# An mLSTM cell followed by a GELU MLP: weights converted by three VectorE operations from 16-bit fields, the first down projection as seven block products, and a new order for the first stage

## The chip, the cores and the metric

The kernel runs on one core of one Trainium2 chip. The metric is the time of one execution on the device in microseconds (us), the median of several runs. The engines named below are TensorE (PE; its weight loads are PEld), VectorE (DVE), ScalarE (ACT), GpSimd (POOL) and SyncE (SP), whose queue issues all the transfers (DMAs).

## The reference, cut to what matters

The gated recurrence is computed for 4 batches, 8 heads, 768 positions and 40 channels. Its output, turned to 3072 tokens of 320 channels, goes through two matrices with an exact GELU between them. The two weight matrices arrive as 64-bit floats; everything else is 32-bit.

```
for t in range(S):                                  # S = 768
    m_new = max(f_gate[t] + m, i_gate[t])
    C = exp(f_gate[t] + m - m_new) * C + exp(i_gate[t] - m_new) * outer(v[t], k[t])
    n = exp(f_gate[t] + m - m_new) * n + exp(i_gate[t] - m_new) * k[t]
    y[t] = sigmoid(o_gate[t]) * (C @ q[t]) / max(|n . q[t]|, 1)
x   = y as (3072, 320)
out = gelu(x @ w_in) @ w_out                        # w_in 320 x 2048, w_out 2048 x 320, float64
```

## The kernel before, in words

The 768 positions are cut into NCH = 6 chunks of 128. A chunk of all 4 batches makes 512 tokens, and these pass through three steps: the cell (class `Cell`, once for each chunk and batch), the up projection with GELU into the hidden tile `g` (2048 x 512), and the down projection (`po`) to the output. Nothing is scheduled automatically: every engine works through its own queue in the order in which the program issues. That order is written out by hand as strings of step names, `FRONT` for the first stage and `DOWN` for each later one, and `play` (L946) runs the steps of a string one by one.

FRONT covers everything up to the end of the first down projection: the gates, the cells of chunks 0 and 1, the conversion of all weights, and the up and down projections of chunk 0. Its names stand for these steps; small letters are for chunk 0 and capitals for chunk 1, with the batch as the number:

- E and N compute the gates of chunk 1 and of chunks 2 to 5 (`gates_of`, L249: scans and differences on VectorE) and turn them with TensorE (`gates_turned`, `decays_of`).
- P fetches a weight piece (`fetch`, L337), L loads q and k, O loads v and the output gate, and B loads the running maxima of a batch (`load_M`).
- w (exponentials on ScalarE, L433), t (transposes of k and q, L482), s (scores, L508, multiplied on VectorE, L511), c (carry, L546), v (values, L622), g (sigmoid of the output gate, L439), y (finish, L635 to L640) and x (transposes of the result, L657, copied to `first_x`, L662) are the parts of a cell. `twice` (L646) copies the last 64 channels into a tile that all batches share.
- A and U are the up projection of the first and the second 256 tokens, in blocks of two hidden tiles (`up_step`, L753, its matmuls L762 and L768, its GELU L772). F is the first down projection: 16 steps, one for each 128 rows of w_out, each with 4 matmuls of 128x320 (L869).
- k (`warm`, L213) and I (`keep_clock`, L381) issue matmuls whose results nobody reads (L216, L387).

The weights are cut into 26 pieces, 10 of w_in (512 values in each partition) and 16 of w_out (320). They pass through NB = 4 shared buffers `bits`. Step K (`conv_one`, L349) splits a piece on VectorE into exponent (L358), upper significand (L363) and whole significand (L365), while two ScalarE operations make the power of two (L360, L361). Step J (`conv_two`, L367) puts in the sign (L372), multiplies (L375), and fetches the piece that is four further on.

Later stages compute the up projection in a split form (L817, L828) and the down projection as seven block products (`down_steps`, L879, matmuls L892): each of the two 256-token halves of `g`, times halves of w_out, with sums of weight blocks (`weight_sum`, L723, 32 operations L731 in all) and sums of hidden blocks (`hidden_sums`, L744) in place of the eighth product. Before, the weight sums were made in the second stage, because the first one didn't need them.

Buffers `sums` for the hidden sums share their tag with `bits`. The queue of SP issues in program order too, so a transfer whose buffer isn't free holds up all that are behind it.

Of the kernel before, what the change touches and what calls it, by code (L numbers as in the profile page):

```python
# [12 lines left out]
U32 = mybir.dt.uint32  # L13
AF = mybir.ActivationFunctionType
OP = mybir.AluOpType

P = 128

I23 = 2.0 ** 23
# [9 lines left out]
    I2 O0 g0 L0 P0 L1 E k1 t0 P1 P2 k7 w0 N k2 w1 O1 K L2 Q s0 O3 w2 q D k2 d P3 t1 w3 c0 L3 J v0 t2 K K y0 s1 I7 v1  # L29
    I8 O2 J g1 L4 I5 c1 K I1 I2 y1 s2 x0 t3 B4 O4 B5 g2 J x1 s3 v2 c2 L5 y2 H T0 x2 G0 v3 g3 c3 K y3 M1 J L6 J A x3  # L30
    M0 K W0 O7 K A O6 O5 J M2 W1 S0 C0 K J J T1 U U K L7 V0 K T2 r J J A G2 K G1 Y0 W2 S1 K M3 C1 A J S2 J K W3 K V1 C2
    Y1 T3 J J U U S3 V2 K K J G3 J Y2 C3 X0 K V3 J K F J F K K B8 F J K F F J K F F F R0 X1 J J K F J F K X2 F J K F
    J Y3 K F R1 J F Z B9 B10 F X3 R2 Z R3 F p"""
# [6 lines left out]
def kernel(  # L40
# [179 lines left out]
    nc.vector.memset(e_hi, 1151.0 * I23)  # L220
    nc.vector.memset(e_lo, 255.0 * I23)

# [74 lines left out]
    def second_gates():  # L297
        gates_of(1, 2)
        nc.sync.dma_start(out=M_d[0], in_=M[:, 1])
        gates_turned((a[:, 1:2], aT[:, 1:2]))  # L300
        decays_of(0, 2, 0, 1)

    def later_gates():
        gates_of(2, NCH)
        nc.sync.dma_start(out=M_d[1:].rearrange("c p l -> p c l"), in_=M[:, 2:])
        gates_turned((a[:, 2:], aT[:, 2:]))
        decays_of(2, NCH - 1, 1, NCH - 1)
# [3 lines left out]
    for name, w in (("in", moe_w_in), ("out", moe_w_out)):  # L311
        rows, cols = w.shape
        w_src[name] = bass.AP(tensor=dataclasses.replace(w.tensor, shape=[rows, 2 * cols], dtype=U32), offset=0,
                              ap=[[2 * cols, rows], [1, 2 * cols]])
# [3 lines left out]
    w_cols = lambda e, f, n: slice(DFF * e + 2 * f, DFF * e + 2 * (f + n))  # L318
# [18 lines left out]
    def fetch(i):  # L337
        if i >= len(pieces):
            return
        src, dst = pieces[i]  # L340
        n = sum(x.shape[0] * x.shape[1] for x in src) // (2 * P)
        bits[i] = raw.tile([P, WP, 2], U32, name="bits", tag="bits", bufs=NB)[:, 0:n, :]
        to = bits[i].rearrange("p n two -> p (n two)")
        row = col = 0
        for x in src:
            nc.sync.dma_start(out=to[row:row + x.shape[0], col:col + x.shape[1]], in_=x)
            row, col = (row + x.shape[0]) % P, col + (x.shape[1] if x.shape[0] == P else 0)

    def conv_one(i):  # L349

        if i < len(pieces):
            n = bits[i].shape[1]
            lo, hi = bits[i][:, :, 0], bits[i][:, :, 1]
            s = sig[i] = raw.tile([P, WP], F32, name="sig", tag="sig")[:, 0:n]
            p = pow2[i] = raw.tile([P, WP], F32, name="pow", tag="pow")[:, 0:n]
            su, pu = s.bitcast(U32), p.bitcast(U32)

            nc.vector.tensor_scalar(out=pu, in0=hi, scalar1=20, scalar2=0x7FF,  # L358
                                    op0=OP.logical_shift_right, op1=OP.bitwise_and)
            nc.scalar.activation(out=p, in_=pu, func=AF.Relu, scale=-I23, bias=e_hi)  # L360
            nc.scalar.activation(out=pu, in_=p, func=AF.Relu, scale=-1.0, bias=e_lo)  # L361

            nc.vector.tensor_scalar(out=su, in0=hi, scalar1=0xFFFFF, scalar2=0x100000,  # L363
                                    op0=OP.bitwise_and, op1=OP.bitwise_or)
            nc.vector.scalar_tensor_tensor(out=s, in0=lo, scalar=2.0 ** -32, in1=su, op0=OP.mult, op1=OP.add)  # L365

    def conv_two(i):  # L367

        if i < len(pieces):
            hi, p = bits.pop(i)[:, :, 1], pow2.pop(i)  # L370
            pu = p.bitcast(U32)
            nc.vector.scalar_tensor_tensor(out=pu, in0=hi, scalar=0x80000000, in1=pu,  # L372
                                           op0=OP.bitwise_and, op1=OP.bitwise_or)
            dst, s = pieces[i][1], sig.pop(i)
            nc.vector.scalar_tensor_tensor(out=dst, in0=s, scalar=2.0 ** -20, in1=p, op0=OP.mult, op1=OP.mult)  # L375
            fetch(i + NB)
# [16 lines left out]
    class Cell:  # L393
# [138 lines left out]
        def carry(self, b):  # L532

            c, n = self.c, self.c * B + b
            qT = self.qT.pop(b)
# [96 lines left out]
        def finish(self, b):  # L632
# [9 lines left out]
            if len(self.finished) == len(self.turned) + 1:  # L642
                self.twice(b)
# [4 lines left out]
        def turn_y(self, b):  # L648
# [10 lines left out]
            if len(self.finished) > len(self.turned):  # L659
                self.twice(b + 1)  # L660
# [74 lines left out]
    class Hidden:  # L735


        def __init__(self, summed):
            self.t = gp.tile([P, NF, TG], F32, name="g", tag="g")
            if summed:  # L740
                self.s1, self.s2 = [[raw.tile([P, HF // 2, HT], F32, name="sums", tag="bits", bufs=NB)
                                     for _ in range(2)] for _ in range(2)]
# [10 lines left out]
    def up_step(g, sets):  # L753

        banks = []
        for k, (i0, i1, t0, t1) in sets:
            banks.append([ps_mm.tile([P, i1 - i0, t1 - t0], F32, name="pu", tag="ab"[k % 2]) for e in range(2)])
# [16 lines left out]
    ups, tags_next = [], []  # L774

    def first_up_steps(h):

        def step(k):
            ups.append((len(ups) + len(tags_next) % 2, (2 * k, 2 * k + 2, HT * h, HT * h + HT)))
            if len(ups) == 2:  # L780
                first_up()

        return [lambda k=k: step(k) for k in range(HF // 2)]

    def first_up():
        if len(ups) == 1:
            tags_next.append(1)
        if ups:
            up_step(first_g, ups)
        ups.clear()  # L790

# [66 lines left out]
    def first_down_steps(g):  # L861
        po = []

        def row(f):

            if f == 0:
                po.extend(ps_mm.tile([P, DM], F32, name="po", tag="ab"[b // 2]) for b in range(B))
            for b in range(B):
                nc.tensor.matmul(po[b], g.t[:, f, b * L:(b + 1) * L], w_out[:, f, :], start=(f == 0),  # L869
                                 stop=(f == NF - 1))  # L870
                if f == NF - 1:
                    if b % 2 == 0:
                        o_sb = outp.tile([P, 2, DM], F32, name="o_sb", tag="o_sb")
                    nc.scalar.copy(out=o_sb[:, b % 2, :], in_=po[b])
                    send(0, b, o_sb[:, b % 2, :])

        return [lambda f=f: row(f) for f in range(NF)]

    def down_steps(c, g):  # L879
        A = lambda e, h: lambda j, t: g.t[:, HF * e + j, HT * h + t * L:HT * h + (t + 1) * L]  # L880
        Sm = lambda s: lambda j, t: s[j // (HF // 2)][:, j % (HF // 2), t * L:(t + 1) * L]
# [53 lines left out]
        def p4(pb, tiles=slice(0, 2)):  # L935
            add(block(1, 0)[:, tiles], pb, block(1, 0)[:, tiles])
            for t in range(2)[tiles]:
                send(c, 2 + t, o_sb[1][:, t, :])

        todo = ((A(0, 0), Bm[0][0], 0, True, p1), (Sm(g.s2), T[2], 1, True, p6),  # L940
                (A(1, 0), Bm[1][0], 0, False, p2), (Sm(g.s1), T[1], 2, True, p5),
                (A(0, 1), T[3], 3, True, p7), (A(1, 0), Bm[1][1], 2, False, p3),
                (A(1, 1), T[4], 3, False, p4))
        return [lambda x=x, t=t: product(*x[0:4], t, x[4]) for x in todo for t in range(2)], sum_late

    def play(order, steps):  # L946

        for word in order.split():
            if word[0] not in "AU":
# [65 lines left out]
```

## Time and profile before

| what | value |
|---|---|
| runs of the kernel before | 479.59, 479.76 and 481.75 us, median 479.76 |
| span of the profiled execution | 479.6 us (it isn't timed apart from that; the span lies 0.2 us below the median of the runs) |
| instructions | 13238 |
| engines busy | PE 469.0, PEld 405.3, DVE 349.1, ACT 222.1, POOL 74.7 us |
| mean granted TensorE clock | 0.999 |
| data moved | 44.57 MB in 170428 packets |

The span runs from the first to the last instruction. An engine's busy time is the time in which it had an instruction under way; matmuls overlap, so a busy PE need not be one at its peak. The chain of waits follows the work that ended last back from the end of the program, and what lies on it sets the time.

### The profile page before, as it was taken

To read this page: it belongs to the slowest core of one execution; us is meant where nothing else is said; L and a number is where in the kernel's file an instruction comes from. 1 tells how busy PE (TensorE), PEld (TensorE's weight loads), DVE (VectorE), ACT (ScalarE), POOL (GpSimd) and SP (SyncE) were. 2 spreads that over 40 slices of the span, in tenths; PEclk is the share of its full clock that TensorE was granted. 3 is DMA by queue.
4 is the path that set the end of the run, shared out by engine and by line. 5 is a ranking of instruction groups with operands and counts; after the bars stand their busy time and mean duration, and the time that the engine had idled before them with its cause. 6 is when DMAs were issued, how large, how long until landed. Compare 5 with 4: busy or idle time off the path is not lost.

```text
span 479.6 us, 13238 instructions
## 1 busy us (share of the span) xinstructions
PE 469.0 (98%) x5380; PEld 405.3 (85%) x5380; DVE 349.1 (73%) x762; ACT 222.1 (46%) x477; POOL 74.7 (16%) x104
## 2 busy tenths in 40 slices
PE   7899999999999999999999999999999999999997
PEld 7787888777777998977999977998977899977997
DVE  7899789797879989956598846597765589724321
ACT  6987999844532942113952113952104862112300
POOL 3002200000020215300224300315300114000000
PEclk9999999999999999999999999999999999999999
DMA  9997966279420348551357551358551350100001
GB/s 176 201 225 172 200 164 149 77 197 194 133 30 4 40 84 189 77 113 12 42 104 178 72 108 15 37 88 178 73 122 15 38 88 8 55 1 0 1 1 55
DMA packets 170428, 44.57 MB, mean 93 GB/s; under 512 B 156448, under 2 KB 163904, under 8 KB 170368
## 3 DMA queue, kind: packets, MB, share of 16 engines
q1 hardware_dynamic: 170368, 43.73, 46.0%
q8 instruction: 42, 0.69, 0.6%
q14 instruction: 18, 0.15, 0.1%
HBM read 39.58 MB, written 4.13 MB: 91 GB/s over the span
## 4 chain that ended last, share of the span: by engine, by line
PE 93%; DVE 3%; SPq 1%; DMA 1%; issue 1%; ACT 0%; DVEq 0%
PE po L892 33%; PE pu L817 24%; PE po L869 7%; PE pu L828 6%; PE pu L762 6%; PE ph L622 4%; PE ps L524 2%; PE px L657 2%; PE pu L768 2%; PE pf L579 2%; PE pf L590 1%; PE ps L508 1%; SPq L148 1%; PE pf L546 1%; PE pt L482 1%
## 5 line engine op out<-in xcount | busy, mean ns | idle before, releaser
L892 PE MATMUL po<-w_out,g 128*128 128x160 f32 x640 | 92.1, 301 | 0.0
L892 PEld LDWEIGHTS po<-w_out,g 128*128 128x128 f32 x640 | 87.6, 190 | 2.3 <-ACT g L832 1.8
L832 ACT ACTIVATE g<-pu 128x512 f32<-128x512 f32 x80 | 40.8, 614 | 52.9 <-PE pu L828 52.8
L892 PE MATMUL po<-w_sums,sums 128*128 128x160 f32 x320 | 47.7, 303 | 0.0
L892 PEld LDWEIGHTS po<-w_sums,sums 128*128 128x128 f32 x320 | 44.1, 190 | 0.7
L817 PE MATMUL pu<-x_hi,w_in_hi 128*128 128x512 f32 x160 | 41.7, 403 | 0.0
L817 PE MATMUL pu<-x_lo,w_in_lo 128*128 128x512 f32 x160 | 40.6, 395 | 0.0
L433 ACT ACTIVATE W<-W,aT 128x128 f32<-128x128 f32 x128 | 39.2, 389 | 0.1
L667 ACT ACTIVATE x_hi<-px 128x384 fp32r<-128x384 f32 x20 | 9.8, 489 | 63.1 <-PE px L657 63.1
L817 PEld LDWEIGHTS pu<-x_hi,w_in_hi 128*128 128x128 f32 x160 | 28.5, 188 | 9.4 <-ACT g L832 4.1
L749 DVE TENSOR_TENSOR sums<-g 128x512 f32<-128x512 f32 x20 | 13.8, 688 | 30.8 <-ACT g L832 30.8
L817 PEld LDWEIGHTS pu<-x_lo,w_in_lo 128*128 128x128 f32 x160 | 30.1, 188 | 7.2
L869 PE MATMUL po<-w_out,g 128*128 128x320 f32 x128 | 35.2, 433 | 0.0
L869 PEld LDWEIGHTS po<-w_out,g 128*128 128x128 f32 x128 | 24.0, 190 | 9.6
L832 ACT ACT_TABLE_LOAD x5 | 6.4, 1283 | 55.1 <-DMA blocks<-in_k_dram 27.6
L817 PE MATMUL pu<-x_all,w_mid 128*128 128x512 f32 x80 | 31.6, 395 | 0.0
L817 PE MATMUL pu<-x_all,w_in_mid 128*128 128x512 f32 x80 | 31.6, 395 | 0.0
L721 DVE TENSOR_TENSOR w_in_mid<-w_in_hi,w_in_lo 128x512 fp32r<-128x512 f32 x20 | 13.8, 688 | 24.5 <-PE pu L817 24.5
L445 POOL MEMSET g<- 32x1024 f32 x8 | 7.6, 945 | 148.1 <-ACT W L433 122.5
L407 POOL TENSOR_SCALAR_AFFINE_SELECT W<-W 128x1024 f32<-128x1024 f32 (+2 forms) x20 | 21.1, 1068 | 53.7 <-DMA W<-M_d 40.9
L762 PE MATMUL pu<-first_x,w_in 128*128 128x256 f32 x128 | 28.9, 381 | 0.0
L905 DVE TENSOR_TENSOR o_sb<-po,o_sb 128x320 f32<-128x320 f32 (+1 forms) x27 | 12.5, 463 | 20.8 <-PE po L892 16.7
(183 smaller groups left out, 908.0 us busy)
## 6 DMA issues: line engine op xcount, KB each, us to landing
W<-M_d SPq DMA_DIRECT2D x16, 512.0 KB, 5.4
bits<-in_moe_w_in_dram SPq DMA_DIRECT2D x20, 256.0 KB, 4.3
bits<-in_moe_w_out_dram SPq DMA_DIRECT2D x16, 320.0 KB, 3.3
ob<-in_o_gate_dram SPq DMA_DIRECT2D x24, 160.0 KB, 3.6
out_dram<-o_sb SPq DMA_DIRECT2D x24, 160.0 KB, 2.1
vb<-in_v_dram SPq DMA_DIRECT2D x14, 160.0 KB, 4.9
kb<-in_k_dram SPq DMA_DIRECT2D x14, 160.0 KB, 5.1
g<-M_d SPq DMA_DIRECT2D x4, 512.0 KB, 4.4
```

What stands on the lines that cost most here:

```text
L407: nc.gpsimd.affine_select(out=x, in_=x, compare_op=OP.is_ge, fill=1.0e30, base=base, pattern=[[0, H], [1, x.shape[2]]], channel_multiplier=-1)
L433: nc.scalar.activation(out=W[n][:, h, :], in_=src, func=AF.Exp, scale=-1.0, bias=aT[:, self.c, r:r + 1])
L622: nc.tensor.matmul(ph[r, h, :], Pm[:, h, r], vb[turn_of(n)][:, h, :], start=True, stop=True)
L721: nc.vector.tensor_tensor(out=w_mid[i], in0=w_hi[i], in1=w_lo[i], op=OP.add)
L749: nc.vector.tensor_tensor(out=s1, in0=a21, in1=a22, op=OP.add)
L762: nc.tensor.matmul(banks[-1][e][:, i - i0, :], in_tile(i, x)[:, e, i % 2 * P:(i % 2 + 1) * P], first_x[:, x, t0:t1], start=(x == 0 and i = ...
L817: nc.tensor.matmul(pus[i][e], w[k][:, e, i * P:(i + 1) * P], x[:, k, :], start=(n == 0 and k == 0), stop=False, skip_group_check=True)
L828: nc.tensor.matmul(pu[e], w[r, i // 2, i % 2 * P:(i % 2 + 1) * P], x[r, NX, :], start=False, stop=(n == 2), skip_group_check=True)
L832: nc.scalar.activation(out=g.t[:, HF * e + i, :], in_=pu[e], func=AF.Gelu, scale=4097.0)
L869: nc.tensor.matmul(po[b], g.t[:, f, b * L:(b + 1) * L], w_out[:, f, :], start=(f == 0), stop=(f == NF - 1))
L892: nc.tensor.matmul(bank[at][:, i, :], lhs(j, t), rhs(j), start=(first and i == 0 and j == 0), stop=(i == n - 1 and j == HF - 1), skip_grou ...
L905: nc.vector.tensor_tensor(out=to, in0=pb, in1=x, op=OP.add)
```

## The change

All three parts lie in the first stage, and what they need of the second is taken out there.

The conversion. A piece is now fetched as 16-bit fields, two bytes past the start of its buffer. In this way the top field (sign, exponent and 4 bits) can be read as one signed 16-bit number, and the next 32 bits as one 32-bit word. Four steps do a piece: a (`conv_zero`: one ScalarE operation), b (`conv_low`: one VectorE operation with one source, written straight into the destination), K (`conv_one`: a VectorE operation with two sources, then one on ScalarE) and J (`conv_two`: one VectorE operation that joins the two parts). VectorE has three operations for each piece instead of five, and ScalarE two, as before. `fetch` is no longer part of J: P appears in FRONT for each piece.

The first down projection. It uses `down_steps` as all later stages do: 14 steps F with 8 matmuls of 128x160 each, instead of 16 with 4 of 128x320. The weight sums (l) and the hidden sums (e, n) of the first stage are now made in FRONT.

The order. Gates are computed chunk by chunk (Ga, Na2 to Na5), loads are split (Lk, Lq, Lv, Lo), `twice` is a step of its own (z, zz), the batches of chunk 0 run in the order 0, 1, 3, 2, the first up blocks run as A, A, U, U, A, and k and I are gone from FRONT; the 12 matmuls of `warm` ahead of FRONT stay. (A 32-bit matmul leaves two records in the trace.)

The core of the diff:

```diff
-    I2 O0 g0 L0 P0 L1 E k1 t0 P1 P2 k7 w0 N k2 w1 O1 K L2 Q s0 O3 w2 q D k2 d P3 t1 w3 c0 L3 J v0 t2 K K y0 s1 I7 v1
-    I8 O2 J g1 L4 I5 c1 K I1 I2 y1 s2 x0 t3 B4 O4 B5 g2 J x1 s3 v2 c2 L5 y2 H T0 x2 G0 v3 g3 c3 K y3 M1 J L6 J A x3
...
+    Ga Na2 P0 Lk0 Lq0 Lv0 Na3 Lk1 a w1 Na4 t0 Lq1 Lv1 Lo3 Lk3 w0 Lo0 Gc Gd s0 t1 b Lq3 w3 Gb D c0 c1 Lo2 Lo1 Lv2 g0
+    Na5 Lk2 s1 Lv3 g2 K Nc v0 g1 v1 t3 y0 g3 Lq2 P1 z0 w2 s3 P2 t2 P3 B4 y1 a v3 c2 Nd b P4 J K x0 d z1 s2 x1 Q a a v2
+    Lk4 M0 b J K K Lv4 Lq4 P5 P6 W0 a y2 J q A z2 y3 T0 K b x2 c3 b z3 x3 J J S0 a K a P7 b J a b K K A P8 a P9 a b M2
+    Nb H P10 J J b b P11 K a K J b a P12 K a J J b K K b C0 V0 J P13 a P14 P15 U K J P16 b b b b a J Lq5 K Lk6 P17 P18
+    J a a Lq6 K K J a K b J a J K U P19 l a b P20 Lk5 l l l J K a P21 a b J K b b K Lv6 P22 P23 P24 P25 Lv5 B5 T2 J J
+    P26 l Lq7 l b a a K b Lo4 M1 K e A P27 Lo5 b b e Lo7 Lv7 Lk7 T1 J a a W1 J K K G3 e G0 F S1 l F e J J l l Y0 M3 C1
+    V1 r l G1 W2 S2 F T3 W3 Y1 F Lo6 C2 G2 V2 P28 S3 l l zz0 F Y2 C3 V3 Y3 P29 F X0 Z Z l F n zz1 l l l F R0 X1 zz2 F
+    B9 R1 X2 B10 zz3 F F F X3 R3 B8 R2 F F p"""
...
-        bits[i] = raw.tile([P, WP, 2], U32, name="bits", tag="bits", bufs=NB)[:, 0:n, :]
-        to = bits[i].rearrange("p n two -> p (n two)")
+        words = raw.tile([P, 2 * WP + 2], U32, name="bits", tag="bits", bufs=NB)
+        to = words.bitcast(U16)[:, 1:1 + 4 * n]
+        bits[i] = words[:, 1:1 + 2 * n].rearrange("p (n two) -> p n two", two=2)[:, :, 0], \
+            words.bitcast(I16)[:, 4:4 + 4 * n].rearrange("p (n four) -> p n four", four=4)[:, :, 0]
...
+    def conv_zero(i):
...
+            nc.scalar.activation(out=s, in_=top, func=AF.Relu, scale=-1.0, bias=e_lo)
...
+    def conv_low(i):
...
+            nc.vector.tensor_scalar(out=pieces[i][1].bitcast(U32), in0=bits[i][0], scalar1=2.0 ** -13, scalar2=2.0 ** 19 - 1.0,
+                                    op0=OP.mult, op1=OP.min)
...
     def conv_one(i):
...
-            nc.vector.tensor_scalar(out=pu, in0=hi, scalar1=20, scalar2=0x7FF,
-                                    op0=OP.logical_shift_right, op1=OP.bitwise_and)
-            nc.scalar.activation(out=p, in_=pu, func=AF.Relu, scale=-I23, bias=e_hi)
-            nc.scalar.activation(out=pu, in_=p, func=AF.Relu, scale=-1.0, bias=e_lo)
-            nc.vector.tensor_scalar(out=su, in0=hi, scalar1=0xFFFFF, scalar2=0x100000,
-                                    op0=OP.bitwise_and, op1=OP.bitwise_or)
-            nc.vector.scalar_tensor_tensor(out=s, in0=lo, scalar=2.0 ** -32, in1=su, op0=OP.mult, op1=OP.add)
+            nc.vector.scalar_tensor_tensor(out=s, in0=top, scalar=LOW, in1=s, op0=OP.max, op1=OP.subtract)
+            nc.scalar.activation(out=p.bitcast(I32), in_=s, func=AF.Identity, scale=2.0 ** 19, bias=e_hi)
...
     def conv_two(i):
...
-            nc.vector.scalar_tensor_tensor(out=pu, in0=hi, scalar=0x80000000, in1=pu,
-                                           op0=OP.bitwise_and, op1=OP.bitwise_or)
-            nc.vector.scalar_tensor_tensor(out=dst, in0=s, scalar=2.0 ** -20, in1=p, op0=OP.mult, op1=OP.mult)
-            fetch(i + NB)
+            nc.vector.tensor_tensor(out=dst, in0=pow2.pop(i).bitcast(U32), in1=dst, op=OP.bitwise_or)
...
-                nc.tensor.matmul(po[b], g.t[:, f, b * L:(b + 1) * L], w_out[:, f, :], start=(f == 0),
-                                 stop=(f == NF - 1))
...
+    def first_sums(f):
+        if f == 0:
+            first_g.sums()
+        hidden_sums(first_g, f, f + 2)
+    def weight_sums():
+        for n in range(1, 5):
+            yield from weight_sum(n)
+    def first_down():
+        yield from down_steps(0, first_g)[0]
+    def late_first():
+        for i in range(2):
+            a12 = first_g.t[:, HF + HF // 2 * i:HF + HF // 2 * (i + 1), 0:HT]
+            nc.vector.tensor_tensor(out=a12, in0=a12, in1=first_g.s2[i], op=OP.subtract)
...
-        up(g, weight_sum(1) + weight_sum(2) + weight_sum(3) if c == 1 else [], [lambda b=b: (steps["K"](b), steps["Q"](b)) for b in range(2)] if steps else [])
-        if c == 1:
-            later = weight_sum(4)
+        up(g, [], [lambda b=b: (steps["K"](b), steps["Q"](b)) for b in range(2)] if steps else [])
```

## The prediction

> **What bounds the kernel now.** I read the page first, for the engines' shares:
>
> ```profile
> PE 469.0 (98%) x5380; PEld 405.3 (85%) x5380; DVE 349.1 (73%) x762; ACT 222.1 (46%) x477; POOL 74.7 (16%) x104
> PE 93%; DVE 3%; SPq 1%; DMA 1%; issue 1%; ACT 0%; DVEq 0%
> ```
>
> The second line is the chain that ended last: 93% of the span is TensorE work, so the question is where TensorE is not yet on it, and what its part there consists of. The chain in order of time tells both:
>
> ```profile
> 26.37 1.21 DVE W L511 x2
> 27.62 1.02 PE ph L622 x28
> ...
> 40.87 3.65 PE pu L762 x16
> ...
> 92.89 0.63 issue
> 93.80 17.42 PE po L869 x64
> ...
> 111.56 4.31 PE po L869 x16
> 116.19 10.77 PE po L869 x40
> ...
> 127.29 2.16 PE po L869 x8
> 129.44 11.16 PE pu L817 x48
> ...
> 445.80 30.64 PE po L892 x224
> ```
>
> Up to 27.6 us the chain runs through gates, a transfer and VectorE. Then TensorE takes over; the first up block starts at 40.87, and the first stage ends at 129.44. In the 88.6 us between these two TensorE waits for almost nothing. The first down projection takes 17.42 + 4.31 + 10.77 + 2.16 = 34.7 us there, and the last line is the same product done as seven block products: 30.6 us.
>
> Then I read the engines by stretches of 10 us (length, then busy us of PE, PEld, DVE, ACT and POOL, the granted clock, the DMA share and GB/s):
>
> ```profile
> 10.00:20.00 10.00, 8.77 (x85) 6.72 (x84) 8.32 (x25) 8.35 (x28) 0.00 (x0) 1.00 1.04 191
> 20.00:30.00 10.00, 9.62 (x146) 8.42 (x148) 9.68 (x22) 9.37 (x22) 0.00 (x0) 1.00 1.01 216
> 30.00:40.00 10.00, 9.04 (x151) 7.90 (x151) 9.06 (x23) 6.19 (x14) 0.00 (x0) 1.00 1.06 257
> ```
>
> VectorE is the busy one here (it idles 2.9 of these 30 us), and part of TensorE's busy time is the unread matmuls. So ahead of the first up block VectorE's queue sets the time, and behind it TensorE does. VectorE's share is mostly conversion:
>
> ```profile
> L365 DVE SCALAR_TENSOR_TENSOR sig<-bits,sig 128x320 f32<-128x320 uint32 x16 | 7.9, 493 | 0.5
> L358 DVE TENSOR_SCALAR pow<-bits 128x320 uint32<-128x320 uint32 x16 | 5.1, 320 | 0.1
> ```
>
> In the timeline an instruction starts before its predecessor's recorded end, so I count from start to start: 0.24 us for an operation with one source on 320 values (0.33 on 512), 0.41 and 0.61 with two sources.
>
> **The first part, up to the first up block.** It now stands on TensorE behind cell 0's four scores and values (L511, L622), but ahead of carry 3 and transposes x2 and x3; its first half needs the second converted piece. What VectorE has queued up to that: it is at 6.6 us when the first chunk's gates are split, as before. Then five chunks of gates one by one, 6.6 us (the lone chunk took 6.62 to 7.96; the last lacks one operation; before, four were done together, and the five took 6.0); turned copies and decays 3.0; four scores of 1.20 = 4.8; two finishes of 1.56 with the shared copy = 3.4; three weighted values of 0.41 = 1.2; and of the conversion three b, two K and two J, 3 x 0.33 + 4 x 0.61 = 3.4. That is 22.4 us. For waits I add 3.0, the idle time of the stretches above, since the same ScalarE exponentials and sigmoids stand in between. So the first up block starts at 6.6 + 22.4 + 3.0 = 32.0 us instead of 40.9. Its second half needs the third piece: two K, one finish and one J more, 3.4 us, so 35.4; the first half takes 3.5, and nothing is lost. Without waits it would start at 29.0.
>
> The order of loads has fetch 0 ahead of k and q of batch 0; these 0.5 MB delay them by some 2 us at the 191 GB/s above. Scores 0 run at 16.7 us today and are due at about 12.5, behind exponentials that need the gates, so this hides; if it doesn't, it costs at most the 2 us.
>
> **The second part, from there to the stage's end.** TensorE had 88.6 us. The seven products take 30.6 instead of 34.7: -4.0. Transposes of chunk 1's batch 0 (1.02), x2 (0.36) and carry 3 (0.47), which stood ahead, now stand behind: +1.9. So 86.5 us, if VectorE follows. Two places where it doesn't:
>
> Carry 3 waits for the weighted values of batch 3, which VectorE reaches behind finish 3, a K, a b and small copies: 35.4 + 3.9 = 39.3; TensorE is there at 37.9. Cost 1.4 us; all of chunk 1 is queued behind it.
>
> The third block product needs sums over all of w_out and all hidden sums, so all 26 pieces must be through by then. From 35.4 on VectorE has 23 b (7 x 0.33 + 16 x 0.24), 22 K (6 x 0.61 + 16 x 0.41) and 23 J (7 x 0.61 + 16 x 0.41) = 27.2 us; twelve hidden sums of 0.61 = 7.3; sixteen weight sums, which took 0.245 each at L731, = 3.9; and cell work (finish 3, four weighted values, two scores, one carry and values, copies) = 8.6. That makes 47.0. From 40 to 130 us VectorE idled 13.6 of 90 us, but often with nothing urgent; I take 10% for its waits on ScalarE and TensorE, 4.7: 87.1 us. TensorE has 50.9 us of work between the two places, so it is there at 32.0 + 1.4 + 50.9 = 84.3 and waits 2.8. Behind that, 33 us of TensorE face 29 of VectorE (remaining sums, adds, cells, splits), so TensorE leads again.
>
> End of the stage: 32.0 + 86.5 + 1.4 + 2.8 = 122.7 instead of 129.4, a gain of 6.7 us.
>
> **The rest.** ScalarE keeps two operations a piece and loses table loads, because the GELUs stand together: 15 loads of 1.28 us in the first stage become 8. It isn't on the path, so I count nothing; it is cover for the steps a. The second stage loses its 32 weight sums from VectorE. It takes 72.8 us today, the third one 71.8 without them: a gain of 0 to 1.0, and I take 0.5. Later stages are unchanged.
>
> Sum: 479.6 - 6.7 - 0.5 = 472.4 us of span; the runs' median lies 0.2 above the span, so 472.6 us.
>
> **What the trace doesn't show.** Step b is arithmetic on every second 32-bit word. L358, of one source too and with the same stride, runs at 0.24 and 0.33; the upper bound is the two-source rows, 0.41 and 0.61. I take L358. Step K reads 16-bit numbers eight bytes apart; the nearest row is L365 (two sources, one strided), which I take for both ends.
>
> **Rivals.** *VectorE binds* (chance 0.18): b goes at the two-source pace. Then 3 x 0.28 ahead of the first block and 7 x 0.28 + 16 x 0.17 = 4.7 us behind it are added where VectorE is already last: 478.1 us. For it: VectorE's margin is gone. Against it: L358's row.
>
> *VectorE keeps up everywhere* (0.20): the two stalls of 1.4 and 2.8 us vanish, 468.4 us; without the start's waits too, 465.4. For it: TensorE lost almost nothing after 40.9 before, with 52 us of conversion on VectorE from start to start (10 x 2.5 + 16 x 1.7); now it is 33 (10 x 1.55 + 16 x 1.06).
>
> *The clock falls* (0.08), the case that ends slower. Steps k and I are gone, 28 unread matmuls (56 records) between 7.5 and 31 us. The granted clock is 1.00 in every stretch, but with them in place. The work of cell 0 on TensorE between 7.4 and 32 us comes to about 21 us at full clock; at half of it 21 us are added, of which the 4 us of gaps hide some, so up to 17. With half of the stretch at half clock the first up block moves by 8.5 us, to 40.5, and the time is 481.1. It decides from a shift of 7.2 us on. The Trainium skill, "TensorE: Matmul & The Clock Gate", Part 1, says that after an idle window of about 3.4 us the array runs at half its clock until such a window was busy; by that rule the case needs a gap of that length. Against it: by my sum 21 of 25 us are work, and the 12 of `warm` at the start remain.
>
> *The transfers slow down* (0.04): rows now land two bytes off a word. Rows of vb land four bytes off kb's alignment at 4.9 against 5.1 us, so no cost shows, but two bytes aren't shown. DMA is busy 100.8 of the first 130 us. The pieces are 10.5 MB, at 3.4 us a MB (the stretch from 100 to 110 us, mostly pieces: 1.89 MB in 6.4 us of busy time) 36 us. At twice that the stage can't end before 137 us: 487. It decides from a factor of 1.8.
>
> That the change doesn't do what it says I leave at no chance: the order of the instructions shows it.
>
> **How the numbers follow.** The forecast itself has 0.47 and spans 469.5 to 475.5. A remaining 0.03 is for waits in the new order that I overlooked, which make it slower. The measurement can tell some 0.5%, 2.4 us, from no change. Faster than 477.4: 0.47 + 0.20 + half of the first rival = 0.76. Same: the other half, 0.09. Slower: 0.08 + 0.04 + 0.03 = 0.15. The range reaches from 465.4 to past the first rival, 479.0.
>
> **What would show it.** In the new profile: first up block (L763) near 32 us, the third block product near 87, the second stage's first matmul near 123; the first down product's matmuls adding up to 30.6; b at 0.33 and 0.24 from start to start; clock 1.00 throughout. Wrong would be: a clock below 1 in the first 40 us, VectorE or a weight transfer as releaser for more than some 8 us of TensorE's waits behind the first up block, or a gap ahead of it past 36 us.

## The result, and the profile after

| what | before | forecast | after |
|---|---|---|---|
| median of the runs, us | 481.31 (20 runs, 479.52 to 482.83) | 472.6 | 479.39 (20 runs, 477.63 to 482.17) |
| span of the profiled execution | 479.6 | 472.4 | 478.2 (its own time: 480.07) |
| first up block starts | 40.87 | 32.0 | 31.15 |
| third block product starts | none | 87.1 | 87.97 |
| second stage starts | 129.44 | 122.7 | 126.44 |
| from there to the last stage's first matmul | 287.8 | 287.3 | 289.5 |

A block product is here one of the 14 steps F, two to each of the seven products; the third is the first one that needs sums. The starts of the stages and the 40.87 are read from the chain, the 31.15 and 87.97 from the timeline, which starts a group 0.1 to 0.4 us earlier (40.80, 129.04 and 126.17 us for the other three).

The ratio of the times is 0.9963 with a 95% interval of 0.9948 to 0.9979: about 0.4% faster, where 1.5% was forecast. The interval only just excludes no change, and of the forecast fall of 7.2 us (479.76 to 472.6) 1.9 came. The time lies 0.4 us above the top of the range.

The page of the changed kernel, first the engines, then the chain that ended last:

```profile
PE 460.5 (96%) x5420; PEld 405.4 (85%) x5420; DVE 338.2 (71%) x735; ACT 211.3 (44%) x468; POOL 75.7 (16%) x104
PE 62%; issue 17%; DVE 8%; ACT 7%; DMA 2%; POOL 2%; SPq 1%; POOLq 0%; DVEq 0%; ACTq 0%
```

TensorE's share of the chain falls from 93% to 62%. Not all of that is waiting: in the fifth stage the chain leaves TensorE at a single wait of 1.4 us, at 399 us, and runs for 63 us (from 336.8) through transfers, GpSimd and ScalarE, while TensorE was busy without a break up to that wait (61.0 us from 337 to 398). The plainer sign is that TensorE has 8.5 us less to do, but the span is only 1.4 us shorter: waits have taken the place of work. The waits of TensorE from 30 us up to the second stage say for whom (engine and line, the releaser, us in total, times, longest; one of the four for W, 0.2 us, lies just ahead of the first up block):

```profile
PE px L655 <- DVE y_rest L644: 3.0, 2, 2.7
PE ph L620 <- DVE W L509: 1.5, 4, 0.6
PE pf L544 <- DVE vw L493: 1.2, 1, 1.2
PE pu L763 <- ACT g L773: 0.7, 1, 0.7
```

In the kernel before this list had a single entry, of 0.6 us. The table by stretches of 10 us (busy us of PE, PEld, DVE, ACT and POOL, granted clock, DMA share, GB/s) puts the largest wait behind 110 us:

```profile
90.00:100.00 10.00, 9.44 (x168) 8.66 (x167) 9.70 (x29) 5.42 (x17) 1.11 (x1) 1.00 0.63 123
100.00:110.00 10.00, 9.15 (x145) 8.64 (x141) 9.02 (x27) 3.13 (x6) 0.74 (x1) 1.00 0.32 52
110.00:120.00 10.00, 7.78 (x57) 7.57 (x58) 6.27 (x17) 0.98 (x2) 0.00 (x0) 1.00 0.76 158
```

From 110 to 120 us both engines idle, TensorE 2.2 us and VectorE 3.7 us. That is no lack of throughput but an order. TensorE's timeline there:

```profile
108.81 0.38 PE L655 MATMUL px<-ident,ob 128*128 128x128 f32 x2
111.89 0.33 PE L655 MATMUL px<-ident,y_rest 128*128 128x128 f32 x1 [2.70 <-DVE y_rest L644]
```

And VectorE's, in the same microseconds:

```profile
107.67 1.29 DVE L713 SCALAR_TENSOR_TENSOR w_in_lo<-w_in_hi,w_in 128x512 fp32r<-128x512 f32 x2 [0.69 <-ACT w_in_hi L711]
108.88 0.56 DVE L729 TENSOR_TENSOR t<-w_out,w_sums 128x160 f32<-128x160 f32 x2
109.35 2.35 DVE L936 TENSOR_TENSOR g<-g,sums 128x1024 f32<-128x1024 f32 x2
111.62 0.22 DVE L644 COPY y_rest<-ob 128x128 f32<-128x128 f32 x1
```

TensorE transposes the output of a batch in three pieces; the third comes from y_rest, a single tile that VectorE fills for one batch after the other (`twice`, steps zz). The copy for batch 1 takes 0.2 us and has been possible since the transposes of batch 0 ended at 104.5 us. But FRONT puts it behind two weight splits (Z), a pair of weight sums (l) and the late hidden differences (n, 2.35 us). The splits wait 0.69 us for ScalarE, which makes w_in_hi only behind a copy of a finished product (L880, at 106.30 us). The last sums are due at 122 us, the differences at about 117, the splits at 126; the copy, due at 109, comes last.

The conversion did what the rows of before promised (line, operation, shape, count, busy us, mean ns, idle before):

```profile
L359 DVE TENSOR_SCALAR w_out<-bits 128x320 uint32<-128x320 uint32 x16 | 4.8, 321 | 1.4 <-DMA bits<-in_moe_w_out_dram 1.4
L367 DVE SCALAR_TENSOR_TENSOR sig<-bits,sig 128x320 f32<-128x320 int16 x16 | 7.6, 488 | 1.0 <-ACT sig L354 1.0
```

b (L359) runs at the pace of the old L358 (320 ns) and K (L367) at that of the old L365 (493 ns).

### The profile page after: what moved, and what is told of

Same layout as the page of the kernel before. It is cut to its first block, busy times and chain, and to the rows that moved or that the text cites. A ratio compares the mean times of both kernels' runs of the same rounds, so it can differ in the third digit from the quotient of the medians.

```text
span 478.2 us, 13344 instructions
## 1 busy us (share of the span) xinstructions
PE 460.5 (96%) x5420; PEld 405.4 (85%) x5420; DVE 338.2 (71%) x735; ACT 211.3 (44%) x468; POOL 75.7 (16%) x104
## 3 DMA queue, kind: packets, MB, share of 16 engines
q1 hardware_dynamic: 170368, 43.73, 47.2%
## 4 chain that ended last, share of the span: by engine, by line
PE 62%; issue 17%; DVE 8%; ACT 7%; DMA 2%; POOL 2%; SPq 1%; POOLq 0%; DVEq 0%; ACTq 0%
PE po L857 30%; PE pu L800 19%; PE pu L811 5%; PE ph L620 2%; PE ps L522 2%; ACT pow L368 2%; PE pf L588 1%; SPq L164 1%; DVE sig L367 1%; PE pf L577 1%; ACT sig L354 1%; DMA g<-M_d 1%; PE px L655 1%; ACT g L773 1%; DMA bits<-in_moe_w_out_dram 1%
## 5 line engine op out<-in xcount | busy, mean ns | idle before, releaser
L857 PE MATMUL po<-w_out,g 128*128 128x160 f32 x768 | 110.8, 301 | 0.3 <-ACT g L773 0.3
L857 PEld LDWEIGHTS po<-w_out,g 128*128 128x128 f32 x768 | 105.2, 190 | 3.1 <-ACT g L815 1.8
L857 PE MATMUL po<-w_sums,sums 128*128 128x160 f32 x384 | 57.0, 303 | 0.0
L857 PEld LDWEIGHTS po<-w_sums,sums 128*128 128x128 f32 x384 | 52.9, 190 | 0.8
L750 DVE TENSOR_TENSOR sums<-g 128x512 f32<-128x512 f32 x24 | 16.5, 687 | 32.9 <-ACT g L815 32.9
L870 DVE TENSOR_TENSOR o_sb<-po,o_sb 128x320 f32<-128x320 f32 (+1 forms) x32 | 15.0, 468 | 28.2 <-PE po L857 24.1
L763 PE MATMUL pu<-first_x,w_in 128*128 128x256 f32 x128 | 28.9, 382 | 0.7 <-ACT g L773 0.7
L857 PE MATMUL po<-t,g 128*128 128x160 f32 x192 | 27.7, 299 | 0.0
L763 PEld LDWEIGHTS pu<-first_x,w_in 128*128 128x128 f32 x128 | 23.9, 190 | 4.5 <-ACT g L773 1.3
```

The costliest lines, as they stand in the source:

```text
L750: nc.vector.tensor_tensor(out=s1, in0=a21, in1=a22, op=OP.add)
L763: nc.tensor.matmul(banks[-1][e][:, i - i0, :], in_tile(i, x)[:, e, i % 2 * P:(i % 2 + 1) * P], first_x[:, x, t0:t1], start=(x == 0 and i = ...
L857: nc.tensor.matmul(bank[at][:, i, :], lhs(j, t), rhs(j), start=(first and i == 0 and j == 0), stop=(i == n - 1 and j == HF - 1), skip_grou ...
L870: nc.vector.tensor_tensor(out=to, in0=pb, in1=x, op=OP.add)
```

## Experiments

The theory after this reading (**order**): conversion and products are worth what was forecast, but VectorE's queue behind the third block product serves late work first, and TensorE's transposes wait for it. Its rivals: VectorE simply has too much to do there (**load**), the block products don't pay, the two-byte offset slows the transfers, the clock. Each run has its own runs of before beside it; their medians lie between 480.4 and 481.1 us.

**The queue's order** (`tail_order`). The same steps; behind the sixth step F the copies zz come first:

```diff
-    ... F X0 Z Z l F n zz1 l l l F R0 X1 zz2 F
-    B9 R1 X2 B10 zz3 F F F X3 R3 B8 R2 F F p"""
+    ... F X0 zz1 R0 Z F F X1 zz2 n F
+    B9 l l R1 X2 B10 zz3 l l Z F F F X3 R3 B8 R2 F F p"""
```

> The changed kernel with the same steps, but behind the third block product VectorE's queue is put in another order: the copies y_rest of batches 1 and 2 (zz1, zz2) come right behind the transposes that free the shared tile, ahead of the two weight splits (Z), the late hidden differences (n) and the last four pairs of weight sums (l). Theory 'order': VectorE is busy for only 29.4 of the 38.2 us behind that product, but TensorE waits 2.7 and 0.3 us for y_rest behind work that is due later; with the copies first both waits go, the second stage starts at 123.4 us instead of 126.4 (between 122.6 and 124.2), and the time falls by 3 us, to 476.4. Theory 'load': VectorE has too much to do there in any order; the waits move to the late sums or the input splits, the second stage starts at 125.5 us or later and the time stays within 1 us of 479.4.

Measured: 474.75 us (474.41 to 476.48), ratio to before 0.989 (0.9869 to 0.9911); the second stage starts at 122.07 us. VectorE's timeline now has the copy at once, the differences behind the next copy:

```profile
105.96 0.22 DVE L644 COPY y_rest<-ob 128x128 f32<-128x128 f32 x1
108.49 0.22 DVE L644 COPY y_rest<-ob 128x128 f32<-128x128 f32 x1
108.62 2.35 DVE L936 TENSOR_TENSOR g<-g,sums 128x1024 f32<-128x1024 f32 x2
```

No wait for y_rest is left, and behind the third block product TensorE waits 0.5 us in all instead of 3.6: order, not load. The second stage starts 4.4 us earlier instead of 3.0; of the rest, 0.7 us is a wait for a GELU that this execution doesn't have (below). This version beats both kernels: 1.1% faster than before, and by the two ratios 0.7% faster than the changed one.

**The conversion alone** (`conv_only`), in the kernel before, with the old order, the old products and the unread matmuls. The steps are those of the change; a, b and K are issued together:

```diff
...
-                 K=in_turn(lambda i=i: conv_one(i) for i in n_pieces), ...
+                 K=in_turn(lambda i=i: (conv_zero(i), conv_low(i), conv_one(i)) for i in n_pieces), ...
```

> The kernel before with the new conversion alone (16-bit fields, three VectorE operations and two of ScalarE), in the old order of steps, with the old products and the unread matmuls. Each piece costs VectorE 0.94 us less (weights in) or 0.65 us less (weights out), but the second VectorE operation now waits for a ScalarE operation of the same piece. Theory 'VectorE sets the start, TensorE the rest': with some five pieces ahead of the first up block, that block starts 3 us earlier, at about 38 us (36.5 to 39.5), and the rest of the stage takes its 88.6 us as before: the time is 478.3 (477 to 480). Rival 'the conversion carries the front's whole gain': the first up block starts at 33 us or earlier and the time is below 474. Second rival 'the wait for ScalarE eats it': the first up block at 40 us or later, the time 481 or more.

Measured: 499.0 us, ratio 1.0391 (1.0363 to 1.0418); first up block at 52.1 us. All but the second rival are refuted, and that one was priced far too low. What VectorE waits for ahead of that block, from 14 to 52 us:

```profile
DVE sig L372 <- ACT sig L359: 13.7, 4, 5.4
```

Not 0.7 us a piece: the ScalarE step stands behind eight exponentials (2.1 us) and copies, and the whole of VectorE's queue stands behind the operation that waits for it. Some of the loss is clock: 0.66 from 30 to 40 us, behind a TensorE wait of 3.9 us.

**With ScalarE's step a piece ahead** (`conv_ahead`):

```diff
+    def conv_ahead(i):
+        if i not in sig:
+            conv_zero(i)
+        conv_low(i)
+        conv_one(i)
+        if i + 1 in bits:
+            conv_zero(i + 1)
```

> The kernel before with the new conversion in the old order, as in the run with the conversion alone, but with ScalarE's first step of a piece issued one piece ahead, so that VectorE's second operation finds it done. Theory 'the wait for ScalarE made the conversion alone lose': VectorE no longer waits 0.7 us in each piece, the first up block is at 39 to 42 us instead of 52.1, and the time is 478 to 483 instead of 499. Rival 'the old order has no place for ScalarE's steps': the ahead step stands in front of the exponentials in ScalarE's queue, the first up block stays behind 46 us and the time above 490.

Measured: 487.77 us, ratio 1.0129 (1.0106 to 1.0152); first up block at 47.9 us. The block is where the rival has it, the time between the two bands. The same wait, from 14 to 48 us, is halved:

```profile
DVE sig L372 <- ACT sig L359: 6.9, 2, 3.9
```

The change's gain ahead of the first up block thus isn't the conversion's by itself. It came only with the order in which the steps a stand well ahead of K between the exponentials. The prediction called ScalarE "cover for the steps a" and priced it at nothing, which holds only in this order.

**Five operations in the new order** (`five_ops`): b and the joining operation of J are issued twice. (This stands in for the old conversion in the new order, which wasn't run.)

```diff
+            for _ in range(2):
                 nc.vector.tensor_scalar(out=pieces[i][1].bitcast(U32), ...
...
+            for _ in range(2):
                 nc.vector.tensor_tensor(out=dst, in0=p, in1=dst, op=OP.bitwise_or)
```

> The changed kernel with the first and the third VectorE operation of each conversion issued twice (the second time with the same operands), so that a piece costs VectorE 2.5 us (weights in) or 1.7 us (weights out) as in the kernel before. Theory 'VectorE is the bound up to the third block product': three pieces ahead of the first up block add 2.8 us there (at 34 us instead of 31.2), the 23 others add 17 us of VectorE work before the third block product, where VectorE now idles 6.4 of 56.9 us; that product comes 13 to 16 us later (at 101 to 104 us instead of 88), and the time is 492 to 496. Rival 'TensorE is the bound behind the first up block': only the front's 2.8 us and a few of waits are added, the time is 482 to 485.

Measured: 505.54 us, ratio 1.0505 (1.0465 to 1.0546), above both bands. The direction is the first theory's, the size isn't: the first up block started at 39.0 us, and the clock was 0.80 and 0.68 in the stretches from 10 and 20 us. Two parts of it were then run alone, with `range(2 if i < 3 else 1)` (`five_front`) and `range(2 if i >= 10 else 1)` (`five_late`).

> The changed kernel with the first and the third VectorE operation issued twice for the first three pieces alone: 2.8 us more of VectorE ahead of the second half of the first up block. Theory 'VectorE is the bound up to there': the first up block starts at 33 to 34 us instead of 31.2, and with VectorE full behind it all of it stays, the time is 481.5 to 483. Rival 'the clock': the gap of TensorE at 14 us grows from 0.7 us towards the 1.08 us behind which the run with all pieces doubled was granted half the clock from 16 to 26 us; then the same happens here, the first up block comes at 38 us or later and the time is 486 or more.

Measured: 484.99 us, ratio 1.0078 (1.0036 to 1.012); first up block at 39.6 us. The rival clock: 2.8 us of VectorE moved it by 8.4 us. The stretch from 16 to 26 us of this run:

```profile
16.00:26.00 10.00, 10.00 (x121) 9.22 (x118) 4.61 (x13) 5.94 (x13) 0.00 (x0) 0.50 1.14 208
```

And TensorE's gap ahead of it:

```profile
15.45 1.50 PE L547 MATMUL pf<-vw,kb 128*64 128x41 f32 x32 [1.08 <-DVE vw L496]
```

In the changed kernel the same gap is 0.70 us, and the clock stays at 1.00:

```profile
14.60 1.13 PE L544 MATMUL pf<-vw,kb 128*64 128x41 f32 x32 [0.70 <-DVE vw L493]
```

> The changed kernel with the first and the third VectorE operation issued twice for the sixteen pieces of the second weight alone: 16 x 0.65 = 10.4 us more of VectorE between about 50 us and the third block product at 88 us. VectorE idles some 4 us in that stretch. Theory 'VectorE is the bound up to the third block product': that product comes 6 to 9 us later (94 to 97 us), the clock stays at 1.00, and the time is 485 to 488. Rival 'TensorE is the bound there': it comes less than 3 us later and the time is below 482.5.

Measured: 492.8 us, ratio 1.0242 (1.0216 to 1.0268); the third block product at 101.6 us, 13.6 us later for 10.4 us of VectorE work, so VectorE is the bound there and the price is above one for one. TensorE waits 6.8 us for GELUs, and the clock is 0.79 to 0.86 in the four stretches from 70 to 110 us, so part of the price is clock. The margin of the new order on VectorE is used up in both places.

**The gap filled** (`five_front_fill`): four unread matmuls in the gap of `five_front`.

```diff
-    ... s0 t1 b Lq3 w3 Gb D c0 c1 ...
+    ... s0 t1 b Lq3 w3 Gb D I4 c0 c1 ...
```

> The kernel of five_front (the first and third VectorE operation twice for the first three pieces) with four unread matmuls of 128 columns put into TensorE's gap of 1.08 us ahead of the first carry, at 14.4 us. In five_front half the clock was granted from 16 to 26 us behind that gap, and the first up block came at 39.6 us. If the gap lowered the clock there, and not the VectorE work, the clock stays 1.00 with the filler, the first up block starts at 33.5 to 35.5 us, and the time is 481 to 483. If the longer VectorE queue itself costs the 8 us, the first up block stays at 38 us or later and the time near 485.

Measured: 482.23 us, ratio 1.0006 (0.9981 to 1.0031). The same stretch of 10 us:

```profile
16.00:26.00 10.00, 8.97 (x174) 7.81 (x170) 7.32 (x21) 9.68 (x23) 0.00 (x0) 1.00 1.04 192
```

The first up block starts at 34.38 us. By then the clock has fallen all the same, at 33 us, behind another gap (1.94 us, for y_rest), and the block runs to 40.7. So the gap and what it does to the clock cost five of the eight us, and VectorE's longer queue about 3.

**Rows instead of block products** (`rows2`), in the new order with the new conversion. A first form, `rows`, which kept the sums of all four batches open at once, gave no time, because its order deadlocks; `rows2` takes two batches at a time.

```diff
+                nc.tensor.matmul(po[i], g.t[:, f, b * L:(b + 1) * L], w_out[:, f, :], start=(f == 0),
+                                 stop=(f == NF - 1))
...
-        up(g, [], [lambda b=b: ...
+        up(g, weight_sum(1) + weight_sum(2) + weight_sum(3) if c == 1 else [], [lambda b=b: ...
```

> The changed kernel with its new conversion and its order, but the first down projection row by row again (two batches at a time, 16 rows each, in the 14 places of the block products), without the first stage's hidden sums, late differences and weight sums; the weight sums are back in the second stage. TensorE then has 34.6 us of products instead of some 32 with the breaks between them, +2.6 us; VectorE has 7.3 + 7.8 + 2.3 us less. Theory 'VectorE's queue holds the stage back': the waits for y_rest (3.0 us) shrink to below 1 us, the waits for W (1.5 us) go, nothing waits for sums, and the second stage starts at about 124.5 us (123.5 to 125.5) instead of 126.2; the time is 477 to 478.5. Rival 'the products pay as the prediction counted them': the second stage starts at 128 us or later and the time is 481 or more.

Measured: 478.86 us (476.01 to 480.79), ratio 0.9947 (0.9925 to 0.9969); second stage at 127.95 us in the timeline, where the changed kernel has 126.17. The waits for y_rest and for sums are gone as expected, the time stands between the two bands, and it can't be told from that of the block products (0.9963). In the changed kernel's order the seven products thus bring nothing that can be measured; with the tail in order they bring 0.6% (0.989 against 0.9947), of which a part may be what follows. In the profiled execution, 1.9 us above the median, TensorE waits 2.5 us for another reason:

```profile
59.68 6.49 PE L763 MATMUL pu<-first_x,w_in 128*128 128x256 f32 x21 [2.46 <-ACT g L773]
```

A piece of the first weight lands late, ScalarE waits 3.7 us for it at its step a, and the GELUs that free TensorE's bank stand behind it.

**The late piece** (`tail_b3`): `tail_order` with the last reader of piece 3 moved up, so that piece 7 is fetched earlier.

```diff
-    ... y2 J q A z2 y3 T0 K b x2 c3 b z3 ...
+    ... y2 J b q A z2 y3 T0 K x2 c3 b z3 ...
```

> The reordered kernel (tail_order) with one more step moved: the first operation on piece 3 (b, L359) stands ahead of the second half of the first up block instead of behind it. It is the last reader of that piece's buffer, so the fetch of piece 7 can start at 36.8 us, behind the transfers before it, instead of 38.4. In the changed kernel and its variants ScalarE waits 0.7 to 3.7 us for that piece at 44 to 48 us, the GELUs stand behind it, and TensorE waits 0 to 2.5 us for the bank that they free. Theory 'a late piece delays the GELU': the wait for piece 7 falls by 1 us or more, no wait of L763 for a GELU is left, and the time is 473 to 474.5, with a smaller spread. Rival 'memory sets the landing': the piece lands no earlier, the time stays within 0.3 us of 474.75.

Measured: 474.84 us (474.3 to 475.97), ratio 0.9877 (0.986 to 0.9894). ScalarE no longer waits for the piece, and no L763 waits for a GELU, but the operation costs its 0.33 us at the place where VectorE is last: L769 waits 0.5 us, carry 3 1.5 us, and the clock is 0.83 from 40 to 50 us. A wait is exchanged for another, and the time is the same.

**The two-byte offset** (`aligned`):

```diff
-        to = words.bitcast(U16)[:, 1:1 + 4 * n]
+        to = words.bitcast(U16)[:, 2:2 + 4 * n]
...
-            words.bitcast(I16)[:, 4:4 + 4 * n]...
+            words.bitcast(I16)[:, 5:5 + 4 * n]...
```

> The changed kernel with the weights' words landing four bytes instead of two bytes into their buffer; the fields are then read one 16-bit place off, so that the low parts of the numbers are others. All instructions are the same. If the two-byte offset slows the transfers, their median time to landing falls from 5.2 us (weights in) and 3.8 us (weights out) to the 4.3 and 3.3 us of before, the queue's share from 47.2% to 46.0%, and the time by up to 1 us. If it doesn't, all stay within 0.2 us and 0.5%, and the time within 0.2%.

Measured: 479.52 us, ratio 0.998 (0.9958 to 1.0002), against 0.9963 (0.9948 to 0.9979) with the offset. The median landing times are 5.5 and 3.7 us, against 5.2 and 3.8, and the queue's share is 46.6% against 47.2%: no cost of the offset shows. Pieces land later than before (4.3 and 3.3 us) for another reason, perhaps because they are now asked for in a shorter time; that wasn't tried.

**Matmuls that stream little, and the program's blocks** (`shift`, `wide`): `tail_order` with unread matmuls at 36 us.

```diff
+    def shift():
+        cold = ps_h.tile([P, P], F32, name="cold", tag="h")
+        for _ in range(64):
+            nc.tensor.matmul(cold[:, 0:8], w_out[:, 0, 0:P], w_out[:, 0, 0:8], ...
```

> The reordered kernel (tail_order) with 64 short unread matmuls of 8 columns at about 37 us, which cost the front 3 to 6 us and move all later matmuls by 64 in TensorE's program. In the stages behind, TensorE has waits of 0.2 to 1.2 us with no releaser, 3.0 us in all in tail_order, each at a time when an instruction transfer of 16 KB (256 instructions) stands in full queues. If these waits are TensorE's program arriving late, they move to other instructions, about half a page (64 matmuls) away, and their sum changes. If they belong to the work of the stage, they stay at the same instructions (pf L588 and ph L620) with the same sum.

> The reordered kernel with 32 unread matmuls of 128 columns (64 records) at 36 us, in the place where shift has 64 of 8 columns (128 records). There TensorE counted as busy throughout, for 23.8 us, and the granted clock was 0.50 from 40 to 64 us. If the clock follows the columns that stream, it stays at 1.00 here, a record takes 0.2 us, the block 12.8 us, and the second stage starts 9 to 13 us later than in tail_order, at 131 to 135 us. If the clock falls in any long stretch of unread or dependent-free matmuls, it falls here too and the block takes 20 us or more. The later matmuls are moved by half a page of 256 instructions (64 matmul records with as many weight loads), where shift moved them by a whole one: if TensorE's waits without releaser in the later stages come from its program arriving late, they stand at other instructions here; if not, at pf L588 and ph L620 some 55 to 57 us into each stage, as in tail_order.

Measured: `shift` 499.4 us, `wide` 479.63 us (one run each). The 64 matmuls of 8 columns took 23.8 us, the 32 of 128 columns 7.4 us. The rows of the two, from `shift`:

```profile
42.00:44.00 2.00, 2.00 (x11) 2.00 (x11) 0.00 (x0) 0.00 (x0) 0.00 (x0) 0.50 1.07 212
```

and from `wide`:

```profile
38.00:46.00 8.00, 8.00 (x72) 7.86 (x71) 2.31 (x6) 2.15 (x3) 1.09 (x1) 1.00 0.70 212
```

TensorE is busy without a gap in both, and only the one that streams 8 columns a matmul is granted half the clock, from 4 us after its first matmul on. (`wide` was granted half of it too, but from 31.3 to 34.4 us, ahead of its unread matmuls and with no gap above 0.7 us in the 6 us before; its first up block took 4.8 us instead of 3.6.) On the waits without a releaser `shift` says nothing: a 32-bit matmul leaves two records, so 64 of them with their weight loads are 256 instructions, a whole block and not half of one as its expectation has it. `wide` moved the program by half a block. The wait of 1.2 us that `tail_order` has 55 us into the fifth stage is gone there, and that stage takes 69.8 us instead of 71.1 (before: 69.8).

## Why the prediction missed

Up to the third block product the mechanism was right, and the times there were within 1 us, in part by luck; behind it the mechanism failed. The miss of 6.8 us (479.39 against 472.6) is the sum of four terms, less 0.7 us by which the median lies below the profiled execution.

- **The base, 1.7 us.** The prediction set the runs' median 0.2 us above the span. The profiled execution of after took 480.07 us for a span of 478.2, and those of before took 1.9 us more than their spans as well (480.06 against 478.1). The three runs of before that the prediction knew, with a median of 479.76, lay low: twenty have 481.31.
- **Behind the third block product, 2.9 us: the step that failed.** "Behind that, 33 us of TensorE face 29 of VectorE, ... so TensorE leads again" compared sums. (By its own working TensorE's part was 35.6 us, 86.5 less 50.9.) The sums were near: TensorE was busy for 34.6 us and VectorE for 29.5. But in queues served in order a sum says nothing of which work stands at the head when something is due. TensorE had 3.6 us of gaps there, 3.0 of them for a copy of 0.2 us; `tail_order`, with nearly the same sums (34.2 and 29.4), takes 34.7 us for this part instead of 38.2. The order of FRONT was readable before: zz1 stands behind Z Z l F n.
- **Up to the third block product, 0.9 us.** The first up block came at 31.15 us instead of 32.0, its second half at 34.7 instead of 35.4. Then the waits were 3.5 us instead of 4.2 (carry 3: 1.2 instead of 1.4), but TensorE was busy for 53.3 us instead of 50.9, so errors of both signs met here. One term is the products: they were taken as one unbroken run of 30.6 us, and a product between other work takes 2.27 to 2.42 us where an unbroken one takes 2.18. All 14 come to 31.5 us, 0.9 us more; but only two of them stand ahead of the third, which makes 0.4 us here. The prediction gives the 50.9 without its terms, so where the other 2.0 us come from stays open. (A slip without effect: 0.5 MB at 191 GB/s delay the loads by 2.6 us, not 2.)
- **The later stages, 2.1 us.** Waits with no releaser, 3.3 us in after against 1.4 in before, make 1.9 us of it. The gain of 0.5 us in the second stage can't be seen in this execution: the stage takes 73.3 us where the third takes 72.4, but 0.9 us of it are such waits. Whether it was there stays open. The other kernels without weight sums in that stage take 72.0 to 72.7 us for it, no more than 0.1 us above their third, while `conv_only` and `conv_ahead`, which have them there, take 0.9 us more for it than for their third. From second to last stage kernels with the same code behind the first stage took 286.4 to 289.5 us, so much of this can be spread of single executions, and after's profiled one lay at its upper end; 0.7 us comes back in the median.

1.7 + 2.9 + 0.9 + 2.1 - 0.7 = 6.9, but for rounding.

Of the signs named as wrong none showed: the clock is 1.00 in every stretch, and VectorE releases TensorE for 5.7 us of waits behind the first up block, below the 8 us allowed. The allowance was larger than the whole of what the measurement can tell.

The rivals. *VectorE binds* gave a time near the measured one (478.1) for a reason that the rows refute: b kept the one-source pace. *VectorE keeps up* is refuted by the waits. *The transfers slow down* is refuted by `aligned`. *The clock falls* didn't happen in the changed kernel's profile, but was nearer than its 0.08 said. That `five_front` came to 39.6 us, near the 40.5 forecast for half the clock in half of the stretch, is luck: 3.2 of its 8.4 us are VectorE's longer queue, and 5.2 us remain for 10 us at half the clock. The condition was wrong. It was weighed by the share of work (21 of 25 us), and at that place a gap of 1.08 us in place of 0.70 was enough.

The Trainium skill, "TensorE: Matmul & The Clock Gate", Part 1, gives in its table of the two states an idle window of about 3.4 us as the condition for half the clock. These runs differ from that row: half the clock was granted behind a gap of 1.08 us, in `wide` with no gap above 0.7 us in the 6 us before, and in `shift` with no gap at all, while a gap of 1.50 us in `tail_order`, at 23 us, left it at 1.00. The length of a gap alone doesn't decide; what does stays open.

## What to carry to other kernels

Where two engines are close, compare not their sums over a stretch but, wait by wait, what stands ahead of the released instruction in its queue and when that is due; the smallest operation with an early consumer goes first. A conversion with fewer VectorE operations can lose if one of them comes to wait for another engine's queue: here it lost 18 us in the old order, and 7 us with ScalarE's step one piece ahead. Take the base of a forecast from several runs, and count products that are cut up by other work at their cut-up price.

## What was not expected of the hardware

- The granted clock follows something other than TensorE's busy time: 0.50 with matmuls of 8 columns back to back (busy 10.0 of 10 us from 50 to 60 us), 1.00 with those of 128. That it is the streamed columns fits both, and also the narrow matmuls (41 columns) around the gap of `five_front`; only these two widths were tried.
- Four unread matmuls in one gap of 1.08 us took 2.8 us off the time (`five_front` 484.99, `five_front_fill` 482.23) and moved the first up block by 5.2 us.
- TensorE's waits without a releaser, 0.2 to 1.4 us once or twice a stage: the trace has 42 instruction transfers of 16 KB over the span, and a shift of the program by half such a block took the largest wait away, a shift by a whole one didn't. But `five_front_fill`, whose program is moved by 16 instructions, doesn't have it either. The Trainium skill, "Runtime: NRT & Kernel Launch", "Instruction fetch mechanics", says that an engine's program is fetched in blocks of 256 instructions, and that crossing into one is mostly hidden. The waits would fit such blocks coming late, but one run of each shift doesn't settle it.
